# Forgetting attention and a gated feed-forward network: the causal mask made on VectorE, constant products on TensorE up to the first gates, and a new order

## The chip, the cores and the metric

The kernel runs on one core of one Trainium2 chip. The metric is the device time in microseconds of one execution of the whole program, inputs and outputs in the chip's main memory. A core has TensorE (matrix products and transposes, into the accumulation memory PSUM), VectorE, ScalarE, GpSimd and SyncE; the last three issue the transfers here, which run on 16 DMA engines beside the compute engines. In the profile's rows PE is TensorE's products, PEld its weight loads, DVE is VectorE, ACT ScalarE, POOL GpSimd and SP SyncE. Each engine takes its instructions strictly in the order in which the program was written for it.

## The reference, cut to what matters

Attention with a forget gate (8 batches, 8 heads, 576 positions, 64 wide), then a root-mean-square norm and a gated feed-forward network on the 4608 x 512 result:

```python
log_f = np.log(np.clip(f, 0.0001, 1.0))
cum = np.cumsum(log_f, axis=-1)
decay = cum[:, :, :, None] - cum[:, :, None, :]
scores = np.where(causal, -1e9, scale * q @ k.T + decay)      # causal: above the diagonal
attn = softmax(scores)
x = (attn @ v).transpose(0, 2, 1, 3).reshape(4608, 512)
xn = x / np.sqrt(np.mean(x * x, -1, keepdims=True) + 1e-6) * rms_g
g = xn @ w_gate                                               # 512 x 1536
return (g * sigmoid(g) * (xn @ w_val)) @ w_out                # w_out 1536 x 512
```

## The kernel before, in words

**Tiles.** The 576 positions of a batch are four tiles of 128 and a last one of 64. For a tile of queries the kernel turns q and k (on TensorE for the first eight tiles, by a transposing transfer for the others), forms the scores of all eight heads against each key tile (L560), takes the exponential on ScalarE (L600), masks the diagonal tile, multiplies by V (L628) and divides by the sum (L644, L646). The decay is put into V: `Vs` is v times exp(-cum), and the same factor stands as a 65th column for the sum (L531, L532). The factors come from f by a chain at the start: clip (L365), logarithm (L367), running sum on VectorE (L372), exponential (L377), transposes into an accumulation bank (L383), copy to `decT` (L387).

**The mask.** For the tiles of the first group (`FAST`) the mask is added in PSUM ahead of the scores: two products of the identity with `keep` (L571), a 128 x 128 tile that holds 0 up to the diagonal and -1e30 beyond it. `keep` is made by GpSimd at the start (`emit_keep`, L351 and L352). For the other diagonal tiles GpSimd zeroes the exponentials (L608).

**The network.** 36 tiles of 128 tokens make nine groups of 512. Per group 12 gates: eight or four products with w_gate and as many with w_val (L773), tanh (L786), two VectorE steps (L788, L780); then the projection with w_out (L807), a copy out of PSUM (L821) and the store (L829, L838). The first two groups' gates go in halves of two query tiles, so that they start when two tiles are normalized (L679, L686, L699, L706). The last of the 36 tiles is projected in two parts, 384 and 128 columns wide: ScalarE copies the first out, VectorE the second; each part is stored by two transfers, one from SyncE's queue and one from ScalarE's.

**The order.** Nothing is ordered by hand. Each step is a `Unit` with an engine, an assumed duration, a key, what it depends on and which buffers it takes and gives. `Plan.run` plays the program with these assumed durations and has each free engine take the ready unit with the lowest key; the sequence so found is the program's order. `SHIFTS` holds one number per unit; a hundredth of it is added to the unit's key. q, k and weights are loaded from GpSimd's queue (L404, L427, L433), the first four v tiles from SyncE's (L454), later ones from both (L417). At most eight transfers are under way per queue.

**The constant products.** After the third tile of the first group the plan adds ten units with the key 50, each one product of the identity with `keep` into an otherwise unused accumulation bank (L591). With this key TensorE takes one only when nothing else is ready, and `spare = 2` leaves two banks free. Nothing reads what they compute.

Of the kernel before, what the change touches and what calls it, by code (L numbers as in the profile page):

```python
# [9 lines left out]
F32 = mybir.dt.float32  # L10
BF16 = mybir.dt.bfloat16
ALU = mybir.AluOpType
ACT = mybir.ActivationFunctionType
# [890 lines left out]
```

## Time and profile before

| | |
|---|---|
| median of three runs | 374.91 us (373.24, 374.91, 374.98) |
| the profiled execution | 372.92 us, span 371.2 us from its first to its last instruction |
| TensorE's granted clock | 1.000 |
| busy: PE, PEld, DVE, ACT, POOL | 96%, 54%, 62%, 56%, 52% |
| read, written in main memory | 38.16 MB, 9.44 MB |
| first gate product (L773) | 22.46 us after the span's start |
| last projection product (L807) | begins its last twelve at 365.87 us |
| chain that ended last, by engine | PE 83%, DMA 8%, POOL 4%, issue 2% |

A row of the timeline gives the start, the busy time, the engine, the line and what is written from what; in brackets stands how long the engine stood idle before, and what ended that. A row of the waits gives who waited for what: the total in us, how many times, the longest. In the chain of waits each row is a start, a length and the work that the next step waited for. Busy time of TensorE contains the drain of its pipeline, so the sum of its rows is a little more than the time that it stood in anyone's way.

### The profile page before, as it was taken

How to read it: one execution, taken by the hardware profiler on the slowest of the kernel's cores; microseconds unless marked ns; L12 is line 12 of the kernel's file. 1: busy time of each engine (PE TensorE's matmuls, PEld its weight loads, DVE VectorE, ACT ScalarE, POOL GpSimd, SP SyncE). 2: the span in 40 equal slices, each digit the busy share in tenths (PEclk: the TensorE clock that was granted, in tenths of full speed). 3: DMA queues.
4: the chain of work that ended last, by engine and by line, in shares of the span. 5: the costliest groups of instructions: out<-in, count | busy, mean ns of one | idle time of the engine just before them, and what ended most of it. 6: DMA issues, size and time to landing. Idle time of an engine off the chain costs nothing.

```text
span 371.2 us, 8881 instructions
## 1 busy us (share of the span) xinstructions
PE 355.6 (96%) x3539; PEld 201.4 (54%) x3539; DVE 229.4 (62%) x456; ACT 207.8 (56%) x313; POOL 191.2 (52%) x255
## 2 busy tenths in 40 slices
PE   2789999999999989999999999999999999999996
PEld 1567866878554555545554555455444554444443
DVE  5587666787666774775735978646664536777200
ACT  4683666777556857775666658467426633332221
POOL 8885999959988725964743478573000210000000
PEclk9999999999999999999999999999999999999999
DMA  9999999999999995999599499993301030000024
GB/s 112 196 204 201 215 211 152 194 140 146 127 165 195 159 125 123 123 175 140 84 166 190 61 132 158 190 143 70 105 2 57 15 116 30 1 1 2 21 98 107
DMA packets 157017, 45.03 MB, mean 121 GB/s; under 512 B 145520, under 2 KB 151408, under 8 KB 156976
## 3 DMA queue, kind: packets, MB, share of 16 engines
q0 software_dynamic: 81952, 17.83, 56.4%
q1 hardware_dynamic: 74864, 26.51, 38.7%
q8 instruction: 27, 0.44, 0.5%
q10 hardware_dynamic: 160, 0.13, 0.2%
q14 instruction: 14, 0.11, 0.1%
HBM read 38.16 MB, written 9.44 MB: 128 GB/s over the span
## 4 chain that ended last, share of the span: by engine, by line
PE 83%; DMA 8%; POOL 4%; issue 2%; DVE 1%; SPq 1%; ACT 0%; POOLq 0%; ACTq 0%
PE ff L773 45%; PE ff L807 26%; PE sc L560 6%; PE ff L628 6%; DMA qk<-in_k_dram 3%; DMA v<-in_v_dram 2%; DMA wv<-in_moe_w_val_dram 2%; POOL qk L404 2%; POOL Vs L531 1%; PE ff L510 1%; DVE xn L690 0%; PE ff L591 0%; POOL keep L352 0%; SPq L496 0%; PE ff L699 0%
## 5 line engine op out<-in xcount | busy, mean ns | idle before, releaser
L600 ACT ACTIVATE PT<-sc 128x1024 bf16<-128x1024 f32 x100 | 98.5, 1021 | 37.9 <-PE sc L560 34.0
L807 PE MATMUL ff<-wo,hT 128*128 128x512 bf16 (+2 forms) x444 | 104.7, 373 | 0.2
L788 DVE SCALAR_TENSOR_TENSOR ga<-th,ff 128x512 f32<-128x512 f32 x108 | 73.6, 685 | 48.7 <-ACT th L786 45.4
L786 ACT ACTIVATE th<-ff 128x512 f32<-128x512 f32 x108 | 64.3, 599 | 60.5 <-PE ff L773 54.6
L773 PE MATMUL ff<-xT,wv 128*128 128x512 bf16 (+1 forms) x480 | 94.5, 337 | 0.3 <-DMA wv<-in_moe_w_val_dram 0.3
L773 PE MATMUL ff<-xT,wg 128*128 128x512 bf16 (+1 forms) x480 | 93.8, 337 | 0.1
L780 DVE SCALAR_TENSOR_TENSOR hT<-ga,ff 128x512 bf16<-128x512 f32 x108 | 72.3, 684 | 18.6 <-PE ff L773 16.0
L773 PEld LDWEIGHTS <-wg 128*128 128x128 bf16 x528 | 50.1, 98 | 41.2 <-issue 0.2
L773 PEld LDWEIGHTS <-wv 128*128 128x128 bf16 x528 | 49.4, 98 | 39.1 <-DMA wv<-in_moe_w_val_dram 0.5
L807 PEld LDWEIGHTS <-hT 128*128 128x128 bf16 x444 | 40.0, 98 | 40.5 <-issue 0.4
L608 POOL TENSOR_SCALAR_AFFINE_SELECT PT<-PT 128x1024 bf16<-128x1024 bf16 x32 | 36.5, 1145 | 49.0 <-ACT PT L600 48.8
L531 POOL TENSOR_TENSOR Vs<-v,decT 128x512 bf16<-128x512 f32 (+1 forms) x37 | 40.2, 1088 | 27.0 <-DMA v<-in_v_dram 26.4
L821 ACT COPY ores<-ff 128x512 f32<-128x512 f32 (+1 forms) x36 | 21.0, 583 | 36.5 <-PE ff L807 36.5
L628 PEld LDWEIGHTS <-PT 128*128 128x128 bf16 (+1 forms) x960 | 32.4, 103 | 15.3 <-ACT PT L600 2.4
L628 PE MATMUL ff<-Vs,PT 128*128 128x65 bf16 (+1 forms) x960 | 36.2, 195 | 3.1 <-ACT PT L600 1.5
L404 POOL DMA_DIRECT2D qk<-in_q_dram x40 | 35.2, 882 | 0.8 <-POOLq L888 0.8
L404 POOL DMA_DIRECT2D qk<-in_k_dram x40 | 34.8, 872 | 0.7 <-PE ff L773 0.4
L679 POOL TENSOR_TENSOR rs<-ms,mhalf 128x1 f32<-128x1 f32 (+1 forms) x28 | 17.2, 614 | 29.4 <-ACT junk L660 24.3
L560 PEld LDWEIGHTS <-KT 64*128 64x128 bf16 x960 | 23.9, 95 | 15.5 <-issue 14.4
L560 PE MATMUL sc<-QT,KT 64*128 64x128 bf16 (+1 forms) x960 | 32.1, 210 | 0.1
L646 DVE TENSOR_TENSOR x<-ff,rden 128x256 f32<-128x256 f32 x72 | 30.6, 424 | 2.5
L690 DVE SCALAR_TENSOR_TENSOR xn<-x,rs,rgB 128x512 bf16<-128x512 f32 x28 | 23.2, 836 | 12.4 <-POOL rs L679 12.2
(58 smaller groups left out, 163.0 us busy)
## 6 DMA issues: line engine op xcount, KB each, us to landing
out_dram<-ores SPq DMA_DIRECT2D x32, 256.0 KB, 2.5
v<-in_v_dram SPq DMA_DIRECT2D x20, 256.0 KB, 5.4
qk<-in_q_dram POOLq DMA_DIRECT2D x32, 128.0 KB, 6.2
qk<-in_k_dram POOLq DMA_DIRECT2D x32, 128.0 KB, 5.9
v<-in_v_dram POOLq DMA_DIRECT2D x12, 256.0 KB, 6.8
wo<-in_moe_w_out_dram POOLq DMA_DIRECT2D x2, 768.0 KB, 12.4
wg<-in_moe_w_gate_dram POOLq DMA_DIRECT2D x2, 512.0 KB, 12.1
wv<-in_moe_w_val_dram POOLq DMA_DIRECT2D x2, 512.0 KB, 13.0
```

Of the source, the lines that this page charges most:

```text
L404: nc.gpsimd.dma_start(out=T_qk[h.slot][0:n, :].rearrange("p (h d) -> p h d", d=D), in_=src[b, :, p0:p0 + n, :].rearrange("h p d -> p h d"))
L531: eng.tensor_tensor(T_Vs[hv.slot][0:n, j, :, 0:D], T_v32[h.slot][0:n, :, :], bcast(dj, D), ALU.mult)
L560: nc.tensor.matmul(t[:, par, c:c + n], lhsT=kt[r, p, kj * 128:(kj + 1) * 128], rhs=qt[r, p, qi * 128:qi * 128 + n], start=(b, qi) not in FAST,
L600: nc.scalar.activation(T_PT[hp.slot].rearrange("p (a c) -> p a c", a=2), T_sc[h.slot], ACT.Exp, scale=scale)
L608: nc.gpsimd.affine_select(out=d, in_=d, pattern=[[0, 1024 // n], [1, n]], compare_op=ALU.is_ge, fill=0.0, base=0, channel_multiplier=-1)
L628: nc.tensor.matmul(po[i * n:(i + 1) * n, p, :], lhsT=T_PT[h.slot][:, c:c + n], rhs=T_Vs[hold_Vs[x].slot][:, kj, 2 * p + par, :], start=(kj ...
L646: nc.vector.tensor_tensor(d, po[:, :, 0:D], bcast(rden[par], D), ALU.mult)
L773: nc.tensor.matmul(T_ff[h.slot][:, c:c + n], lhsT=w[:, dc, fc * 128:(fc + 1) * 128], rhs=xT[:, dc, t0:t0 + n], start=(dc == 0), stop=(dc = ...
L780: nc.vector.scalar_tensor_tensor(hT, in0=three[0], scalar=0.5, in1=three[1], op0=ALU.mult, op1=ALU.mult)
L786: th = act(0.6, key - 0.1, lambda: nc.scalar.activation(T_th[ht.slot], T_ff[hg.slot], ACT.Tanh, scale=0.5), [ug], take=[ht])
L788: a = dve(0.72, key - 0.1, lambda: nc.vector.scalar_tensor_tensor(T_ga[ha.slot], in0=T_th[ht.slot], scalar=1.0, in1=T_ff[hg.slot], op0=ALU ...
L807: nc.tensor.matmul(T_ff[hf.slot][:, 0:wide], lhsT=T_hT[hold_hT[g].slot][:, fc, j * 128:(j + 1) * 128], rhs=wo[:, fc, cols], start=(fc == 0 ...
```

## The change

`keep` is now made on VectorE: a running sum of the identity's rows along the free dimension gives 1 from the diagonal on and 0 before it, and one further pass takes off 1 and multiplies by 1e30. There are 24 constant products instead of 10; the first becomes ready when `keep` is there, and those that the plan would place after the first gate are planned but not written into the program (`gates_on`). The first part of the last tile's result is copied by VectorE, and both of its stores go through ScalarE's queue. Some assumed durations of the planner are other, and all of `SHIFTS` is new, so the order is new in the whole kernel.

```diff
 SHIFTS = (
-    0, 0, 0, 0, 105, 0, 233, 0, -21, 138, -2, -97, -143, 99, -68, -7, -156, -83, 68, 67, 271, 121, 109, -61, -136,
...
+    192, 80, -10, -64, -70, -114, 28, 12, 26, 20, 201, -61, -93, 228, 95, 185, -84, 23, 386, -127, -102, 35, -147,
...
 )
...
+    upto = sb.tile([128, 128], F32, name="upto")
+    one128 = sb.tile([128, 1], F32, name="one128")
...
     def emit_keep():
-        nc.gpsimd.memset(keep, 0.0)
-        nc.gpsimd.affine_select(out=keep, in_=keep, pattern=[[1, 128]], compare_op=ALU.is_ge, fill=-1.0e30, base=0,
-                                channel_multiplier=-1)
+        ones = bass.AP(tensor=one128.tensor, offset=one128.offset, ap=[one128.ap[0], [0, 128]])
+        nc.vector.tensor_tensor_scan(upto, ones, ident_f, 0.0, ALU.mult, ALU.add)
+        nc.vector.tensor_scalar(keep, in0=upto, scalar1=-1.0, op0=ALU.add, scalar2=1.0e30, op1=ALU.mult)
...
     def emit_ones():
         nc.vector.memset(unit, 1.0)
+        nc.vector.memset(one128, 1.0)
...
-    keeps = pool(0.65, -28.5, emit_keep)
...
+    keeps = dve(0.5, -39.9, emit_keep, [iden_f])
     d3 = dve(1.75, -40, emit_cum, [d2])
...
-            qkload[b, nm, j] = load("POOL", 0.9 * n / 128, (8 * n, 0.0009), key, emit, take=[h])
+            qkload[b, nm, j] = load("POOL", 0.9 * n / 128, (8 * n, 0.00105 if j == 0 and b < WAVE else 0.0009), key, emit, take=[h])
...
-            vload[b, 0] = load("SP", 0.95, (1024, 0.00117), -30 + 0.1 * b, emit, [t])
+            vload[b, 0] = load("SP", 0.95, (1024, 0.00102), -30 + 0.1 * b, emit, [t])
...
-            u = pe(0.42 if b + j * WAVE < 4 else 0.25, key, emit, [iden, qkload[b, nm, j]], take=[h], give=[hq])
+            u = pe(0.42 if b + j * WAVE < 2 else 0.27, key, emit, [iden, qkload[b, nm, j]], take=[h], give=[hq])
...
+    gates_on, go = [], [iden, keeps]
+    for i in range(24):
+        h1 = Hold("ff", 1)
+
+        def fill(h1=h1):
+            if not gates_on:
+                m = bass.AP(tensor=keep.tensor, offset=keep.offset, ap=[keep.ap[0], [0, 4], [1, 128]])
+                nc.tensor.matmul(T_ff[h1.slot], lhsT=ident, rhs=m, start=True, stop=True)
+        go = [pe(0.43 if i < 10 else 0.24, 50, fill, go, take=[h1], give=[h1])]
+        go[0].lat = 0.0
+        go[0].spare = 2
...
-            u = pe(0.86, key - 0.6, bias, [iden, keeps] + ([last_bias[0]] if last_bias[0] else []), take=[h0])
+            u = pe(0.86 if tiles[0][0] < 2 else 0.46, key - 0.6, bias, [iden, keeps] + ([last_bias[0]] if last_bias[0] else []), take=[h0])
...
-        u = pe(0.19 + 0.25 * cols, key, emit, deps, take=holds, give=gives)
+        u = pe(0.19 + 0.25 * cols - (0.1 if tiles[0][:2] in FAST else 0.0), key, emit, deps, take=holds, give=gives)
         last_block[0] = u
-        if len(fast) == 3 and fast[-1] is holds:
-            go = [u]
-            for _ in range(10):
...
-                go = [pe(0.3, 50, fill, go, take=[h1], give=[h1])]
-                go[0].spare = 2
...
-            cost = 1.42 if qi == LAST else 0.03 + (0.12 if qi else 0.22) * (qi + 1)
+            cost = 1.42 if qi == LAST else 0.03 + 0.12 * (qi + 1)
...
-                t = pe(0.25 if g else 0.42, key, tr, [u, iden], take=[hf], give=[hn])
+                t = pe(0.25 if g else 0.27, key, tr, [u, iden], take=[hf], give=[hn])
...
         def mm(w, h):
+            gates_on.append(g)
             xT = T_of[g][hx.slot]
...
-            add, copy = (dve, nc.vector.tensor_copy) if x else (act, nc.scalar.copy)
+            add, copy = (dve, nc.vector.tensor_copy) if halves == 2 else (act, nc.scalar.copy)
...
-                eng, queue = ("ACT", nc.scalar) if j == 3 and i == 1 else ("SP", nc.sync)
+                eng, queue = ("ACT", nc.scalar) if j == 3 and (x == 0 or i == 1) else ("SP", nc.sync)
```

More of the change, by code (lines that the diff above doesn't have):

```diff
@@ L541, in tiles_of @@
         return [(((x, 2 * i), (x, 2 * i + 1)), 64) for x in (b, b + 1) for i in range(2)] + [(((b, LAST), (b + 1, LAST)), 64)]
-    hold_PT, masked, last_block, last_bias, fast = {}, {}, [None], [None], []
+    hold_PT, masked, last_block, last_bias = {}, {}, [None], [None]
     FAST = {(b, qi) for b in range(B) for qi in range(LAST) if home(b, qi)[0] == 0}
@@ L571, in bias @@
                     nc.tensor.matmul(T_sc[h0.slot][:, par, :], lhsT=ident, rhs=m, start=True, stop=False)
-            u = pe(0.86, key - 0.6, bias, [iden, keeps] + ([last_bias[0]] if last_bias[0] else []), take=[h0])
+            u = pe(0.86 if tiles[0][0] < 2 else 0.46, key - 0.6, bias, [iden, keeps] + ([last_bias[0]] if last_bias[0] else []), take=[h0])
             last_bias[0] = u
             deps.append(u)
-            fast.append(holds)
         for b, qi, items, n in tiles:
@@ L581, in score_block @@
         cols = sum(len(items) * n / 128 for b, qi, items, n in tiles)
-        u = pe(0.19 + 0.25 * cols, key, emit, deps, take=holds, give=gives)
+        u = pe(0.19 + 0.25 * cols - (0.1 if tiles[0][:2] in FAST else 0.0), key, emit, deps, take=holds, give=gives)
         last_block[0] = u
-        if len(fast) == 3 and fast[-1] is holds:
-            go = [u]
-            for _ in range(10):
-                h1 = Hold("ff", 1)
-                def fill(h1=h1):
-                    m = bass.AP(tensor=keep.tensor, offset=keep.offset, ap=[keep.ap[0], [0, 4], [1, 128]])
-                    nc.tensor.matmul(T_ff[h1.slot], lhsT=ident, rhs=m, start=True, stop=True)
-                go = [pe(0.3, 50, fill, go, take=[h1], give=[h1])]
-                go[0].spare = 2
         for (b, qi, items, n), h in zip(tiles, holds):
```

152 rows, old and new, of the table SHIFTS are left out of this document.

## The prediction

> **What bounds the kernel now.** I read the page's span, engine rows and slices first, then the chain of work that ended last, the waits of TensorE, TensorE's busy time in stretches, and the timeline of the first 28 us and the last 7.
>
> ```profile
> span 371.2 us, 8881 instructions
> PE 355.6 (96%) x3539; PEld 201.4 (54%) x3539; DVE 229.4 (62%) x456; ACT 207.8 (56%) x313; POOL 191.2 (52%) x255
> PE   2789999999999989999999999999999999999996
> DMA  9999999999999995999599499993301030000024
> ```
>
> TensorE is busy 96% of the span; its thin slices are the first two or three, one near 135 us and the last. The stretches say how much is idle (first number: length; then PE busy; the last three are TensorE's granted clock, the packets in flight on each DMA engine and GB/s):
>
> ```profile
> 22.00:34.00 12.00, 11.06 (x109) 9.55 (x110) 9.40 (x17) 6.80 (x13) 6.86 (x9) 1.00 1.46 205
> 34.00:46.00 12.00, 11.64 (x153) 9.74 (x151) 7.90 (x16) 6.60 (x9) 10.94 (x14) 1.00 1.56 209
> 46.00:130.00 84.00, 84.00 (x1050) 55.47 (x1049) 59.89 (x123) 56.11 (x76) 74.90 (x98) 1.00 1.58 166
> 130.00:140.00 10.00, 8.57 (x156) 5.09 (x155) 7.30 (x17) 5.29 (x7) 2.74 (x4) 1.00 0.85 118
> 140.00:366.00 226.00, 226.00 (x1969) 112.73 (x1962) 131.30 (x242) 119.49 (x190) 76.50 (x95) 1.00 0.64 92
> ```
>
> From 46 to 366 us TensorE has 1.43 us of idle time in all (10.00 - 8.57, around 135 us); from 22 to 46 it has 0.94 + 0.36 = 1.30. So an order can win at most 2.7 us behind 22 us, and the rest must come from the first 22 us or the tail. It can lose without such a limit.
>
> What holds the start is the chain up to 34 us:
>
> ```profile
> 3.91 1.73 POOL qk L404 x2
> 5.64 0.23 POOL keep L351
> 5.93 1.34 POOL keep L352
> 7.52 2.61 POOL qk L404 x3
> 12.47 8.30 DMA wv<-in_moe_w_val_dram
> 20.77 12.93 DMA qk<-in_k_dram
> ```
>
> GpSimd issues the q and k loads, stops to build the mask (0.23 + 1.34), goes on issuing, and from 12.47 the chain is transfers. TensorE's waits name the same things, and the one of 1.4 us near 135:
>
> ```profile
> PE sc L571 <- POOL keep L352: 1.6, 1, 1.6
> PE ff L628 <- POOL PT L608: 1.4, 1, 1.4
> PE ff L510 <- DMA qk<-in_k_dram: 1.2, 2, 0.7
> ```
>
> **Part 1, the mask goes from GpSimd to VectorE.** GpSimd loses 0.23 + 1.34 = 1.57 us ahead of the third pair's loads. Does the DMA stream move by as much?
>
> ```profile
> 4.00:6.00 2.00, 0.61 (x4) 0.45 (x5) 1.21 (x9) 0.86 (x2) 1.93 (x4) 1.00 1.70 108
> 8.00:10.00 2.00, 2.00 (x11) 1.08 (x9) 0.00 (x0) 1.20 (x2) 2.00 (x3) 1.00 1.62 214
> 10.00:12.00 2.00, 1.28 (x15) 1.04 (x15) 0.42 (x1) 0.64 (x2) 2.00 (x4) 1.00 1.94 203
> 20.00:22.00 2.00, 1.29 (x21) 0.81 (x21) 1.49 (x6) 1.89 (x4) 2.00 (x3) 1.00 1.34 206
> ```
>
> ```profile
> 5.13 5.23 SPq L454 DMA_DIRECT2D v<-in_v_dram  x4
> ```
>
> In the hole that the mask leaves (8 to 10 us) the engines still move 214 GB/s: SyncE's four v loads, issued from 5.13 to 10.36, fill it. From 20 to 22 us the rate stands at 206 GB/s, and from 22 to 34 it is 205. So loads issued 1.57 us sooner mostly change places with v loads. Bounds: 0 (fully swapped) and -1.57 us (the whole delay); I take -0.3, nearest to the row of 8 to 10 us, where 1.62 packets are in flight against 1.94 in the next stretch: a sixth of 2 us is spare.
>
> VectorE gains a scan over 128 elements and a pass of 128x128 from f32 to bf16, and one memset:
>
> ```profile
> 4.45 0.34 DVE L363 CAST ident<-ident_f 128x128 bf16<-128x128 f32 x1
> 5.83 1.35 DVE L372 TENSOR_TENSOR_SCAN hT<-unit,hT 64x576 f32<-64x576 f32 x1 [0.72 <-ACT hT L367]
> 12.14 0.49 DVE L387 COPY decT<-ff 128x320 f32<-128x320 f32 x1 [1.63 <-PE ff L383]
> ```
>
> The scan is 1.35 x 128/576 = 0.30, the cast 0.34, the memset of one column little: about 0.7 us, 0.6 to 1.0. VectorE pauses 0.72 us before the long scan, where most of it fits. If it lies ahead of that scan, the decay chain (scan, exp, transposes, decT) is late by up to 0.7; decT waited 1.63 us for TensorE, so that cover holds: 0. Without it the first scaled V would be 0.7 later, and the first tile's values with it. The mask is there at about 6 instead of 7.27, and TensorE's wait of 1.6 us ends about 1.2 sooner. What is late next is the second k tile:
>
> ```profile
> 10.77 0.61 PE L510 MATMUL ff<-ident,qk 128*128 128x128 bf16 x4 [0.72 <-DMA qk<-in_k_dram]
> ```
>
> It was issued ahead of the mask, so it does not come sooner. The 1.2 us are therefore worth 0 by themselves.
>
> The row of the mask shows something else: on GpSimd the 128x128 select of the identity took 0.29 us, and that of the mask 1.34, under VectorE's scan (5.83 to 7.18).
>
> ```profile
> 3.62 0.29 POOL masks.py:199 TENSOR_SCALAR_AFFINE_SELECT ident_f<-ident_f 128x128 f32<-128x128 f32 x1
> ```
>
> The Trainium skill, "SBUF — State Buffer", section "Who interferes with whom", says that a VectorE instruction with two SBUF inputs excludes a GpSimd one that reads SBUF, and that a VectorE cast can hold off the writing of descriptors for GpSimd's own DMAs. The trace agrees with the first (1.34 against 0.29). By the second, the new cast could hold up a q or k issue by its 0.34 us; that speaks against this part, and would turn its -0.3 into 0.
>
> **Part 2, 24 constant products instead of 10, from the mask on, none after the first gate.** Before, three of the ten lay ahead of the gates (19.1 to 21.2) and seven in the last microseconds. TensorE's rate changes once, about 18 us:
>
> ```profile
> 14.51 1.90 PE L571 MATMUL sc<-keep,ident 128*128 128x512 bf16 x4
> 17.18 0.62 PE L510 MATMUL ff<-ident,qk 128*128 128x128 bf16 x4
> 18.31 0.40 PE L699 MATMUL ff<-ident,xn 128*128 128x128 bf16 x4 [0.52 <-ACT xn L686]
> 21.73 0.68 DVE L706 TENSOR_TENSOR xT<-ff,rgT 128x512 bf16<-128x512 bf16 x1
> 22.46 1.03 PE L773 MATMUL ff<-xT,wg 128*128 128x256 bf16 x8
> 27.86 0.39 PE L773 MATMUL ff<-xT,wv 128*128 128x256 bf16 x2 [0.30 <-DMA wv<-in_moe_w_val_dram]
> ```
>
> Four transposes take 0.62 before and 0.40 after, though the granted clock reads 1.00 throughout. The change came after 14.51 to 18 us, some 3.6 us with hardly a pause (an estimate). With fills from 6 us I expect it at 10 to 13 us. Then the four bias products at 14.51 and the two transposes up to 17.80 halve: about 0.85 + 0.4 = 1.25 us of TensorE's queue that the second tile's values wait behind. Against it: a fill that started just before real work delays it by up to one product's step, 1.90 / 4 = 0.47, in perhaps three pauses that matter, on average half of it: +0.7. So I expect the first gate 0.55 sooner than 22.46, between +0.7 (fills only delay) and -1.25. But the product at 27.86 waits for wv, so a gate that starts sooner is caught there. To the end I carry -0.5 (0 to -1.25), part 1's 0.3 being what makes the weights sooner.
>
> The Trainium skill, "TensorE: Matmul & The Clock Gate", section "What's actually happening", says that the array runs at half rate until a window of about 3.4 us has been busy, that the window runs freely, and that where it begins differs from run to run. The rows agree (0.62 against 0.40 after some 3.6 us).
>
> **Part 3, the tail.**
>
> ```profile
> 365.65 0.21 PE ff L591
> 365.87 0.67 PE ff L807 x12
> 366.24 1.30 ACTq L838 DMA_DIRECT2D out_dram<-ores  x2
> 366.63 0.29 DVE L821 COPY ores<-ff 128x128 f32<-128x128 f32 x1 [20.24 <-PE ff L807]
> 365.69 2.40 SPq L838 DMA_DIRECT2D out_dram<-ores  x4
> ```
>
> ```profile
> L821 ACT COPY ores<-ff 128x384 f32<-128x384 f32 x1 | 0.5, 480 | 0.1
> ```
>
> One fill (0.21) goes from before the last products; the six behind them delayed nothing. The 384-wide copy moves to VectorE: 0.29 + 256 x 1.04 ns (the slope of 0.68 us for 512) = 0.56 against 0.48 on ScalarE. SyncE's last issue ended at 368.09; now ScalarE's queue has three of 0.65, from about 366.3 to 368.2. Sum 0, between -0.4 (SyncE's spare issue) and +0.3.
>
> **Part 4, the new order and the planner's new costs.** They change no instruction's work. They can win at most the 2.7 us above, and lose as much per new wait as the 1.4 at 135 us. I take 0, -2.0 to +3.0.
>
> **Sum.** The profiled execution took 372.92 (span 371.2): -0.3 - 0.5 + 0 + 0 = 372.1. The median shown, 374.91, is 2.0 above it; the three runs are 373.24, 374.91 and 374.98, two groups 1.7 apart. One mechanism fits that distance: if the rate rises some 3.6 us later than here, the first gates (1.03 for eight products with the last one's drain) run at half rate from 22.46 to about 26 and half of 3.6, 1.8 us, are lost. Fills up to the first gates take that away. No row shows a late run, so this is an estimate; it makes the median 372.1 plus the 0.3 by which the fastest of the three lies above the profiled execution: 372.4.
>
> **The rivals.**
> *R1: the start is hidden behind the transfers, and the spread stays.* For it: 206 GB/s from 20 to 22, 205 after, and the wait at 27.86. Then -0.7 remains of the median, 374.2: no change that can be told. "The fills don't do what they say" ends here too: transposes still at 0.62 up to 18 us.
> *R2: the order also clears the wait at 135 us and part of 22 to 46.* Worth another 1.4 to 2.7: 370.5. Against it: nothing in the change gives GpSimd less to do there, where it is busy 74.90 of 84 us.
> *R3, the other side: a new wait for GpSimd behind 46 us.* Place: the values products (L628) behind the mask of PT or the scaling of V, when the order puts a load's issue ahead of either. Price 1.4 each, by the row. With the start as in R1 it decides from 2.6 us, that is two such waits: 374.2 + 2.8 = 377.0. For it: GpSimd's 74.90 of 84 leave little room; against it: before had one such wait in 320 us.
> *R4: 24 fills run out ahead of the gates, and the rate falls again in a pause.* Then the first gates run at half rate as in the estimate above, 1.8 on 372.1: 373.9, with R1's result. For it: 24 fills last 24 x 0.47 = 11 us at the slow step and 5 to 6 at the fast one (0.21), and from 6 to 22 are 16 us; against it: the rate held before through the pauses from 18.31 to 22.46 with three fills. That an idle window closes the array's clock is what the Trainium skill, "TensorE: Matmul & The Clock Gate", states in the same section; no row here shows a fall.
>
> **How the numbers follow.** 0.5% is 1.87 us, about what a measurement of this kernel can tell. Forecast 372.4: 0.42. R1 with R4: 0.33. R2: 0.08. R3: 0.17. Faster: 0.08 and nearly all of the forecast's, 0.48; same: 0.35; slower: 0.17. Range: down to 370.4 (R2, the order's -2.0 on the forecast) and up to 376.0, which leaves most of R3 out. The forecast's own range is 371.3 to 373.5.
>
> **What would show it.** Part 1: no GpSimd mask, TensorE's wait for keep gone, VectorE's scan and cast near 0.30 and 0.34, the wv wait near 27.9 earlier by about 0.3. Part 2: four transposes at 0.40 by 13 us, the first gate near 21.9. Part 3: no L591 at the end, ScalarE's queue last. Part 4: TensorE 84.00 of 84 busy again from 46 to 130. Wrong, if the runs keep their two groups, or if a wait over 1 us stands behind 46 us.

## The result, and the profile after

The changed kernel took 376.21 us (median of 11 runs, 373.6 to 377.9) beside 373.55 for the kernel before (11 runs): a ratio of 1.0064, 95% interval [1.0041, 1.0088]. It is slower by 2.4 us (1.5 to 3.3 by the interval), where 372.4 and "faster" were forecast. Ratios here are taken round by round without disturbed runs, so they aren't always the quotient of the medians. The profiled execution took 375.92 us, 3.0 above the one shown of before; its span is 2.2 longer.

The page of the changed kernel, the lines that answer to those shown of before:

```profile
span 373.4 us, 8833 instructions
PE 353.3 (95%) x3495; PEld 201.8 (54%) x3542; DVE 236.7 (63%) x460; ACT 206.9 (55%) x312; POOL 189.5 (51%) x253
PE   3779999999999999999999899999999999999995
PEclk9699999999999999999999999999999999999999
DMA  9999999999899994999999939991421001100304
```

The thin slice of TensorE near 135 us is gone and one near 210 has come. The second slice of the granted clock reads 6. Its waits:

```profile
PE sc L586 <- DVE keep L355: 5.2, 1, 5.2
PE ff L513 <- DMA qk<-in_q_dram: 1.9, 1, 1.9
PE ff L632 <- POOL PT L612: 1.6, 1, 1.6
PE ff L632 <- DVE Vs L535: 0.6, 1, 0.6
```

The lateness begins at the first gates. From the timeline of the changed kernel, VectorE and then TensorE:

```profile
4.45 0.42 DVE L354 TENSOR_TENSOR_SCAN upto<-one,ident_f 128x128 f32<-128x128 f32 x1
4.90 0.23 DVE L355 TENSOR_SCALAR keep<-upto 128x128 bf16<-128x128 f32 x1
5.04 0.88 DVE L367 TENSOR_SCALAR hT<-hT 64x576 f32<-64x576 f32 x1
5.88 0.08 DVE L454 MEMSET v<- 128x1 f32 x4
21.02 0.69 DVE L534 TENSOR_TENSOR Vs<-v,decT 128x512 bf16<-128x512 f32 x1 [1.32 <-DMA v<-in_v_dram]
25.24 0.68 DVE L710 TENSOR_TENSOR xT<-ff,rgT 128x512 bf16<-128x512 bf16 x1
```

```profile
21.86 0.28 PE L632 MATMUL ff<-Vs,PT 128*128 128x65 bf16 x4 [0.56 <-DVE Vs L535]
25.98 1.03 PE L778 MATMUL ff<-xT,wg 128*128 128x256 bf16 x8 [0.22 <-DVE xT L710]
```

The first gate starts at 25.98 instead of 22.46. Behind it stands the last v tile: VectorE idles 1.32 us for it until 21.02, and the second tile's transposed input (L710) comes behind that on the same queue. That v landed at 21.0, in before at 17.94; the last weight landed at 34.77 instead of 32.84, although GpSimd issued the first at 9.34 instead of 10.11. Counting TensorE's weight loads, each with the columns of its product and without the constant products, the changed kernel reaches the same amount of work about 3.4 us later than before behind the first gates (25 us), 2.3 to 3.2 later from 40 to 130 us, 1.3 to 1.6 later from 138 to 207 (before has its own wait of 1.35 for the mask of PT at 136), 2.4 to 2.9 behind its own wait of 1.65 at 210, and 2.2 at the last product. So the lateness of the start, 2.5 us at 40, is about the whole difference of these two profiled executions, and the two waits for a mask of PT nearly cancel. Nothing is lost in the tail:

```profile
368.31 0.98 DVE L826 COPY ores<-ff 128x384 f32<-128x384 f32 x2 [8.22 <-PE ff L812]
368.90 1.85 ACTq L843 DMA_DIRECT2D out_dram<-ores  x3
```

What the transfers did shows in stretches of the start, before and then after (the last three numbers are the granted clock, the packets in flight per DMA engine and GB/s):

```profile
4.00:8.00 4.00, 1.28 (x6) 0.70 (x7) 3.02 (x12) 2.17 (x3) 3.93 (x12) 1.00 1.66 146
8.00:12.00 4.00, 3.28 (x25) 2.12 (x24) 0.42 (x1) 1.84 (x3) 4.00 (x6) 1.00 1.78 208
12.00:16.00 4.00, 3.30 (x31) 2.13 (x28) 2.96 (x10) 2.52 (x3) 3.49 (x5) 1.00 1.80 188
16.00:20.00 4.00, 3.36 (x35) 2.15 (x33) 3.12 (x10) 3.56 (x7) 3.06 (x6) 1.00 1.60 190
```

```profile
4.00:8.00 4.00, 2.82 (x12) 1.53 (x13) 3.21 (x10) 2.01 (x3) 4.00 (x12) 1.00 1.75 116
8.00:12.00 4.00, 2.51 (x27) 1.44 (x24) 1.94 (x7) 3.37 (x6) 4.00 (x6) 1.00 1.54 179
12.00:16.00 4.00, 2.76 (x23) 1.67 (x24) 1.73 (x6) 0.31 (x2) 1.85 (x3) 0.55 1.83 166
16.00:20.00 4.00, 4.00 (x35) 2.52 (x33) 2.16 (x7) 2.63 (x5) 2.50 (x4) 0.60 1.36 183
```

The rate is lower in each: 30 + 29 + 22 + 7 = 88 GB/s for 4 us is 0.35 MB, which at 205 GB/s is 1.7 us, near the 1.93 by which the weights are late. From 16 to 20 us the two queues carry this (GpSimd's q0, mostly weights; q1, mostly SyncE's v), again before, then after:

```profile
q0 software_dynamic: 2062, 0.75, 158.2%
q1 hardware_dynamic: 31, 0.01, 1.5%
```

```profile
q0 software_dynamic: 1043, 0.48, 89.4%
q1 hardware_dynamic: 985, 0.25, 47.0%
```

Before, v was nearly over by then: its last tile landed at 17.94. In the changed kernel v's packets of some 256 bytes go one for one with those of the other queue (985 and 1043).

### The profile page after: what moved, and what is told of

The parts are those of the page before. It is cut to its first block, busy times and chain, and to the rows that moved or that the text cites. A ratio compares the mean times of both kernels' runs of the same rounds, so it can differ in the third digit from the quotient of the medians.

```text
span 373.4 us, 8833 instructions
## 1 busy us (share of the span) xinstructions
PE 353.3 (95%) x3495; PEld 201.8 (54%) x3542; DVE 236.7 (63%) x460; ACT 206.9 (55%) x312; POOL 189.5 (51%) x253
## 4 chain that ended last, share of the span: by engine, by line
PE 71%; POOL 10%; DMA 10%; issue 4%; SPq 3%; DVE 1%; ACT 0%; POOLq 0%; DVEq 0%
PE ff L778 39%; PE ff L812 21%; PE ff L632 5%; PE sc L575 5%; POOL qk L407 5%; DMA qk<-in_q_dram 4%; DMA wv<-in_moe_w_val_dram 3%; DMA v<-in_v_dram 3%; POOL Vs L534 2%; SPq L499 2%; SPq L714 1%; POOL PT L612 1%; POOL v L420 1%; POOL Vs L535 1%; POOL rs L683 1%
## 5 line engine op out<-in xcount | busy, mean ns | idle before, releaser
L812 PE MATMUL ff<-wo,hT 128*128 128x512 bf16 (+2 forms) x425 | 100.1, 373 | 1.4 <-issue 0.5
L778 PE MATMUL ff<-xT,wv 128*128 128x512 bf16 (+1 forms) x465 | 93.5, 335 | 0.8 <-issue 0.2
L778 PE MATMUL ff<-xT,wg 128*128 128x512 bf16 (+1 forms) x469 | 92.6, 336 | 0.9 <-DVE xT L710 0.2
L812 PEld LDWEIGHTS <-hT 128*128 128x128 bf16 x444 | 40.8, 98 | 42.9
L826 ACT COPY ores<-ff 128x512 f32<-128x512 f32 x35 | 20.4, 589 | 32.3 <-PE ff L812 30.3
L694 DVE SCALAR_TENSOR_TENSOR xn<-x,rs,rgB 128x512 bf16<-128x512 f32 x28 | 27.4, 993 | 13.8 <-POOL rs L683 13.7
## 6 DMA issues: line engine op xcount, KB each, us to landing
wo<-in_moe_w_out_dram POOLq DMA_DIRECT2D x2, 768.0 KB, 12.4
```

Source lines behind the costliest of these rows:

```text
L778: nc.tensor.matmul(T_ff[h.slot][:, c:c + n], lhsT=w[:, dc, fc * 128:(fc + 1) * 128], rhs=xT[:, dc, t0:t0 + n], start=(dc == 0), stop=(dc = ...
L812: nc.tensor.matmul(T_ff[hf.slot][:, 0:wide], lhsT=T_hT[hold_hT[g].slot][:, fc, j * 128:(j + 1) * 128], rhs=wo[:, fc, cols], start=(fc == 0 ...
```

## The experiments

Three theories are told apart. M, mixing: GpSimd's old mask was the gap in which SyncE's v loads went through; without it, and with v issued later, v rides beside q, k and the weights. Q: the new order loads the second tile's q fifth instead of third. O: the new order as a whole. Some expectations name more: V, VectorE's scan and cast themselves cost the time; C, the clock; S, a wait near 208 us; N, a cost of the new order in the middle. The code is shortened: `place` and `swap` stand for lines that move steps in the finished order, `...` for lines left out, and the comments are added. The numbers of all kernels, from their traces and runs ("GpSimd pauses" is whether it does other work of about 1.6 us ahead of its later loads; times of landing and of the gate are of one profiled execution each; a_no_fill has six runs, the others 11 or 12):

| kernel | GpSimd pauses | q1 packets, 16-20 us | last v, last weight land | first gate | ratio to before [95%] |
|---|---|---|---|---|---|
| before | yes | 31 | 17.94, 32.84 | 22.46 | 1 |
| after | no | 985 | 21.0, 34.77 | 25.98 | 1.0064 [1.0041, 1.0088] |
| a_v_first | no | 333 | 18.68, 33.78 | 23.88 | 1.0069 [1.0044, 1.0094] |
| a_q1_first | no | 987 | 20.83, 35.15 | 25.86 | 1.0050 [1.0023, 1.0076] |
| a_pool_held | yes | 365 | 18.53, 32.93 | 23.57 | 1.0042 [1.0018, 1.0067] |
| a_start3 | yes | 31 | 17.25, 33.14 | 23.80 | 1.0043 [1.0005, 1.0081] |
| a_no_fill | no | 873 | 20.35, 34.45 | 25.64 | 1.0118 [1.0075, 1.0162] |
| a_gps_mask | yes | 40 | 17.25, 33.09 | 24.41 | 1.0020 [0.9990, 1.0049] |
| b_mask_dve | no | 833 | 19.27, 33.99 | 23.50 | 1.0018 [1.0000, 1.0036] |
| b_mask_dve_held | yes | 91 | 18.33, 33.24 | 22.71 | 1.0008 [0.9978, 1.0038] |
| b_all | no | 854 | 20.00, 33.97 | 24.35 | 1.0061 [1.0032, 1.0090] |
| b_tail | yes | 57 | 17.87, 32.79 | 22.57 | 0.9987 [0.9962, 1.0011] |
| b_fill | yes | 85 | 17.87, 32.80 | 23.08 | 0.9980 [0.9957, 1.0003] |
| b_best | yes | 3 | 16.41, 33.09 | 22.97 | 1.0011 [0.9986, 1.0037] |

**a_v_first**: the changed kernel, with the clip and the four one-column memsets that release v's loads ahead of the mask's scan on VectorE.

```diff
-        for u in P.run():
+        order = P.run()
...
+        place([d1] + early_v, keeps)      # before the mask
+        for u in order:
```

> The changed kernel with VectorE's clip of f and the four one-column memsets that release SyncE's v loads put back ahead of the mask's scan; all else in its order. Theory M (mixing): the v loads, issued 0.85 us later than before and now beside q and k loads, reach into the weights' transfer and slow it; with the v loads back at about 5.1 us the last v tile should land near 20 instead of 21.0, the last w_val near 34.2 instead of 34.8, the end 0.5 us sooner. Theory Q (load order): the second tile's q, loaded fifth and landing at 13.2, sets the first gate at 26.0; it stays fifth here, so the first gate stays within 0.4 us of 26.0 and the time within 0.3 us of the changed kernel.

The start was repaired by 2.1 us at the first gate, and the time not at all: 376.38. The work was 1.4 us late at 40 us, then more was lost near 208. GpSimd's and TensorE's timeline and the stretches there:

```profile
208.22 1.04 POOL L542 TENSOR_TENSOR Vs<-v,decT 128x512 bf16<-128x512 f32 x1 [7.41 <-DMA v<-in_v_dram]
209.35 1.09 POOL L620 TENSOR_SCALAR_AFFINE_SELECT PT<-PT 128x1024 bf16<-128x1024 bf16 x1
210.50 0.57 PE L640 MATMUL ff<-Vs,PT 128*128 128x65 bf16 x13 [2.62 <-POOL PT L620]
```

```profile
208.00:212.00 4.00, 1.50 (x16) 0.81 (x17) 1.11 (x4) 1.43 (x2) 3.40 (x5) 0.89 1.39 167
212.00:216.00 4.00, 4.00 (x49) 2.25 (x48) 2.45 (x6) 1.19 (x3) 0.71 (x1) 0.69 0.17 33
```

A late v holds GpSimd, its next mask comes late, TensorE stands 2.62 us; then the granted clock falls to half for 3.4 us (211.1 to 214.5 in the trace): four 512-wide products take 1.73 us at 210.90, and 1.03 at 206.09.

**a_q1_first**: the second tile's q is loaded third, the third tile's k fifth; their transposes and copies change places too.

```diff
-        for u in P.run():
+        order = P.run()
...
+        swap(order, issues[2, "k", 0], issues[1, "q", 0])     # and turns, copies
+        for u in order:
```

> The changed kernel with the second tile's q loaded third, as before, and the third tile's k fifth, and the two turns on TensorE and their copies moved likewise (the third tile's k is turned just ahead of its q). Theory Q: q lands near 8 instead of 13.2, TensorE's wait of 1.9 us for it goes, the second tile's scores come near 11.5 instead of 15.1, the first gate near 23 to 24 instead of 26.0 (w_gate lands at 22.0), and the end 1.5 to 2.5 us sooner, that is level with before. Theory M: the weights still land as late (last w_val near 34.8), the gates that start sooner wait for them, and the end is at most 0.5 us sooner.

The wait of 1.89 for q went, the first gate did not move; v was as late as ever, and the wait turned up there:

```profile
21.69 0.28 PE L640 MATMUL ff<-Vs,PT 128*128 128x65 bf16 x4 [1.81 <-DVE Vs L543]
25.86 1.70 PE L786 MATMUL ff<-xT,wg 128*128 128x256 bf16 x8
```

Theory Q falls as the cause by itself. The first eight gate products took 1.70 instead of 1.03: the clock had closed at 23.8.

**a_pool_held**: GpSimd is kept busy as before by a memset and a select on a tile that nobody reads.

```diff
+        nc.gpsimd.memset(spare, 0.0)
+        nc.gpsimd.affine_select(out=spare, in_=spare, ...)
         nc.gpsimd.memset(mhalf, -0.5)
...
```

> The changed kernel with GpSimd held for as long as the mask held it before (a memset and a select into a spare tile nobody reads, ahead of its other constants). Theory M: q and k from the fifth load on are issued 1.6 us later, the v loads pass in the gap, the last v lands near 18 to 19 instead of 21.0 and the last w_val near 33 to 33.5 instead of 34.8; the end 1 us sooner although the engine does more. Theory Q: the second tile's q is issued later and lands no sooner than 13.2, first gate 26 or later, end 0 to 1 us later.

To issue the weights later by 0.8 us made them land 1.84 us sooner (32.93 against 34.77), v 2.5 sooner, the gate 2.4 sooner, though again at half rate. That is theory M's sign. The time did not follow: the ratio, 1.0042, is lower than the change's, but the intervals overlap.

**b_mask_dve** and **b_mask_dve_held**: the kernel before with part 1 alone, the mask behind the memsets that release v, so that v is issued on time; and the same with GpSimd held.

```diff
-        nc.gpsimd.memset(keep, 0.0)
-        nc.gpsimd.affine_select(out=keep, in_=keep, ...)
+        nc.vector.tensor_tensor_scan(upto, ones, ident_f, 0.0, ALU.mult, ALU.add)
+        nc.vector.tensor_scalar(keep, in0=upto, scalar1=-1.0, op0=ALU.add, scalar2=1.0e30, op1=ALU.mult)
```

> The kernel before with the mask alone moved to VectorE, behind the memsets that release the v loads; the rest in the order of before (ten constant products, tail as before). The prediction's part 1: -0.3 us (0 to -1.57). Theory M: the gap in GpSimd's issues is gone, v tiles land 1 us or more later than in before (17.9 for the last), the last weight later than 32.8, the end 0.5 to 1.5 us later than before. Theory Q: the load order is that of before, so the first gate is at 22.5 or a little sooner and the end level or up to 0.5 us sooner.

> The kernel before with the mask on VectorE and GpSimd held as long as its mask held it (memset and select into a spare tile). Theory M: the gap in GpSimd's issues is back, v tiles pass in it: last v near 18, last weight near 32.9, time level with before within 0.3 us although VectorE does more. Theory V: VectorE's scan and cast are what costs; then it stays 0.5 to 1 us above before like the kernel with the mask alone moved (1.0018).

This pair is one edit apart, with before's order. The queues from 16 to 20 us, first not held, then held:

```profile
q0 software_dynamic: 1602, 0.50, 112.3%
q1 hardware_dynamic: 833, 0.21, 39.8%
```

```profile
q0 software_dynamic: 2179, 0.73, 159.6%
q1 hardware_dynamic: 91, 0.02, 4.2%
```

A pause of 1.57 us on GpSimd takes v out of the weights' way, and the weights land 0.75 us sooner. Over the table the split has no exception: with a pause the last weight is there by 33.24, without one never before 33.78. So theory M stands for the transfers. It does not follow for the first gate of this pair, which starts 0.8 us sooner when held. The two run level up to 18.5 us, and VectorE waits for no v in either; then one has a closed clock until 22.88 and the other an open one from 18.05, here by the same four transposes, not held and then held:

```profile
18.53 0.61 PE L702 MATMUL ff<-ident,xn 128*128 128x128 bf16 x4 [0.52 <-ACT xn L689]
18.56 0.40 PE L706 MATMUL ff<-ident,xn 128*128 128x128 bf16 x4 [0.51 <-ACT xn L693]
```

That is the clock's part. In time the pair is 1.0018 and 1.0008, which doesn't tell them apart; v issued on time, part 1 costs at most 0.36%. Theory V isn't excluded, but held, with scan and cast on VectorE, it can cost at most 0.38%.

**a_start3**: all three edits of the start in the changed kernel.

```diff
+        place([d1] + early_v, keeps)
...
+        swap(order, issues[2, "k", 0], issues[1, "q", 0])     # and turns, copies
...
+        nc.gpsimd.affine_select(out=spare, in_=spare, ...)    # behind its memset
```

> The changed kernel with all three edits of its start together: v loads released ahead of the mask's scan, the second tile's q loaded third, GpSimd held for 1.57 us by a select into a spare tile. If the start is what costs (theories M and Q), the last v lands near 18, the last w_val near 32.9, the first gate is at 22 to 23 and TensorE's work up to 60 us is level with before within 0.5 us. Theory S: a second cost lies in the new order near 208 us, where values wait for GpSimd's mask behind a late v; by S this wait grows as TensorE comes there sooner (it was 1.8 us in the changed kernel and 4.7 with its clock closing in the kernel with early v loads), so that the time stays 1 to 2 us above before although the start is level. Without S: 374 or less, level with before.

The start is repaired to 0.75 us of work at 40 us, though the first gate, at 23.80, misses the 22 to 23 expected. The time isn't repaired: two waits stand in the middle that the changed kernel's profile does not have. Theory S named another place, near 208 us, and there nothing is lost.

```profile
85.69 1.91 PE L790 MATMUL ff<-xT,wg 128*128 128x256 bf16 x16 [1.81 <-DVE ga L805]
108.35 1.02 PE L790 MATMUL ff<-xT,wg 128*128 128x512 bf16 x4 [2.02 <-DMA xT<-xn]
```

**a_no_fill**: the 13 constant products are left out.

```diff
-    gates_on, go = [], [iden, keeps]
+    gates_on, go = [0], [iden, keeps]
```

> The changed kernel with none of the 13 constant products that it writes into the program; every other instruction in its place. Prediction's part 2: the clock opens later, the first gate comes up to 0.55 us later than with them, time +0 to +0.5. Theory C (clock): the fills opened it at 9.0 in the changed kernel but left a pause in which it closed at 12.4 and opened again at 19.2; without them it opens once, between 17 and 23, and the time is within 0.5 us of the changed kernel. If fills only delay real work: 0.5 us sooner.

```profile
25.64 1.86 PE L778 MATMUL ff<-xT,wg 128*128 128x256 bf16 x8 [1.17 <-DVE xT L710]
```

The clock opened at 30.05 and the gates began at half rate; the work was 4.3 us late at 40 us instead of 2.5. These 1.8 us are the price that the prediction estimated for a late clock, and the times agree (1.0118 against 1.0064, 2.0 us, from six runs; the intervals overlap a little).

**b_tail**: the kernel before with the new tail and without the seven late fills.

```diff
...                                           # no constant products behind the first gate
-            add, copy = (dve, nc.vector.tensor_copy) if x else (act, nc.scalar.copy)
+            add, copy = (dve, nc.vector.tensor_copy) if halves == 2 else (act, nc.scalar.copy)
...
-                eng, queue = ("ACT", nc.scalar) if j == 3 and i == 1 else ("SP", nc.sync)
+                eng, queue = ("ACT", nc.scalar) if j == 3 and (x == 0 or i == 1) else ("SP", nc.sync)
```

> The kernel before with two things alone: the seven constant products behind the first gate are left out, and the last tile's first part is copied by VectorE and stored from ScalarE's queue alone. The prediction said 0 (-0.4 to +0.3). From the two traces the time from the last projection product on is 0.2 shorter and 0.2 of fill goes: -0.4 us, a ratio of 0.999.

0.9987 [0.9962, 1.0011]: no difference. Its profiled execution shows something else. Up to the last microseconds it is the program of before, and yet it lost 3.8 us near 109, where before's profile lost none, and its clock opened at 10.62 instead of 17.87 (and was closed again from 17.45 to 20.86):

```profile
10.96 0.40 PE L510 MATMUL ff<-ident,qk 128*128 128x128 bf16 x4 [0.94 <-DMA qk<-in_k_dram]
22.57 1.03 PE L776 MATMUL ff<-xT,wg 128*128 128x256 bf16 x8
```

So one program can differ by that much from execution to execution, and a wait in the middle of a single profile can't be charged to an edit. The open clock did not make the first gate sooner: 22.57 against 22.46.

**b_all** and **b_fill**: before's order of everything. b_fill has GpSimd's mask, eight more fills set ahead of the early transposes and values, no late ones, and the new tail. b_all has the mask on VectorE ahead of the clip as well, as the change has it, and two fills more.

```diff
...
+        order.remove(keeps)                       # b_all alone
+        order.insert(order.index(d1), keeps)      # b_all alone
+        for ref, n_ in ((turns[1, "q", 0], 2),    # b_all alone
+                        (turns[1, "k", 0], 2), (vals[0, 0][0], 3), (trs[0, 0], 2), (vals[1, 0][0], 1)):
+            # n_ constant products ahead of ref
```

> Everything of the change but its new order: the kernel before, in its own order and load order, with the mask on VectorE ahead of the clip of f (as in the changed kernel), 13 constant products (ten of them put by hand ahead of the turns and values that pause, three as before) and none after the first gate, and the new tail. If the new order costs nothing, this is as slow as the changed kernel, ratio 1.006. Theory O (the order, with its loads, is the larger part): 1.000 to 1.002, that is the mask's +0.9 us of the kernel with the mask alone, less the tail's 0.4.

> The kernel before with its mask on GpSimd, eight more constant products put ahead of the second tile's k turn, the first values and the first transposed tiles, none after the first gate, and the new tail. Theory C: the clock opens by 15 us and is open when the gates start; the start is then set by the weights' transfer as before, so the time is that of the kernel with the tail alone, ratio 0.998 to 0.999, with fewer high runs. If fills delay real work: 1.000 to 1.002.

Run side by side they differ clearly: 1.0061 [1.0032, 1.0090] and 0.9980 [0.9957, 1.0003]. They differ in part 1 and in two fills; b_best, below, has these two fills as well and is level with before. Part 1 as it was made is therefore enough for a loss as large as the change's, without the new order, and the fills and the tail without it lose nothing. VectorE and the first gate of b_all, then the first gate of b_fill:

```profile
17.36 0.70 DVE L542 TENSOR_TENSOR Vs<-v,decT 128x512 bf16<-128x512 f32 x1 [2.38 <-DMA v<-in_v_dram]
24.35 1.03 PE L791 MATMUL ff<-xT,wg 128*128 128x256 bf16 x8
```

```profile
23.08 1.03 PE L788 MATMUL ff<-xT,wg 128*128 128x256 bf16 x8 [0.25 <-DVE xT L720]
```

Theory O, that it takes the new order to lose, falls. The third v tile landed at 17.34 here, at 15.63 in b_mask_dve, where v was issued 0.9 us sooner and VectorE waited for none, and at 12.52 in before: the lost pause and the late issue add up. One thing stays open: the profiled execution of b_all was its fastest, 374.15, and 1.2 us longer in span than before's; where its other runs (median 375.50) lose the rest no trace shows.

**b_best**: b_fill's edits and two fills more, with the mask on VectorE behind the memsets and GpSimd held.

```diff
+        nc.vector.tensor_tensor_scan(upto, ones, ident_f, 0.0, ALU.mult, ALU.add)     # and the pass to keep
...
+        nc.gpsimd.affine_select(out=spare, in_=spare, ...)                            # behind its memset
...
+        for ref, n_ in ((turns[1, "q", 0], 2), ...):                                  # as in b_all
```

> The same with the mask on VectorE behind the memsets that release the v loads and GpSimd held as long as before, with two products more ahead of the second tile's q turn. The mask is there at about 5.7 us, so the clock opens by 11 to 13; v and weights land as in before (theory M). Expected 0.997 to 0.999; the loads still set the first gate at 22 to 22.7.

1.0011 [0.9986, 1.0037]. With the same fills as b_all, it has v on time and the pause, and b_all's loss is gone (the intervals overlap between 1.0032 and 1.0037). No kernel here is clearly faster than the one before; b_fill comes nearest.

**a_gps_mask**: the changed kernel with part 1 alone undone.

```diff
-        nc.vector.tensor_tensor_scan(upto, ones, ident_f, 0.0, ALU.mult, ALU.add)
-        nc.vector.tensor_scalar(keep, in0=upto, scalar1=-1.0, op0=ALU.add, scalar2=1.0e30, op1=ALU.mult)
+        nc.gpsimd.memset(keep, 0.0)               # between its fourth and fifth load
+        nc.gpsimd.affine_select(out=keep, in_=keep, ...)
```

> The changed kernel with its first part alone undone: the mask is made by GpSimd again, between the fourth and the fifth of its loads, and VectorE has neither scan nor cast. The new order of every other step, the 13 fills and the new tail stay. If part 1 is the whole loss (theory M: without GpSimd's gap the v loads ride beside the weights), the last v lands by 18.5 us, the last weights by 33.3, the first gate starts at 22.5 to 23.6 (the second tile's q is still the fifth load, 1.6 us later than in the changed kernel) and the time is 0.998 to 1.001 of before. If the new order costs something of its own in the middle (theory N), the start is repaired in the same way and the time still is 1.003 to 1.005. If neither (the order of the loads alone holds the start), the first gate stands at 25 us or later and the time is 1.006.

```profile
q0 software_dynamic: 1676, 0.77, 146.5%
q1 hardware_dynamic: 40, 0.01, 1.9%
```

v and weights came back as theory M says (17.25 and 33.09). The first gate, at 24.41, is later than expected: the second tile's q still held TensorE 0.95 us at 13.43, so the order of loads has its share once v is out of the way. The work is 0.9 late at 40 us instead of 2.5. The ratio, 1.0020 [0.9990, 1.0049], lies between theory M's and theory N's and decides neither; its interval overlaps the change's.

## Why the prediction was wrong, point by point

**Part 1 is the step that failed.** It was given -0.3, between 0 and -1.57, from the row of 8 to 10 us at 214 GB/s: "loads issued 1.57 us sooner mostly change places with v loads". The swap was seen, the sign of its price not. An exchange was taken to cost nothing at worst ("0 (fully swapped)"). But the bytes went through more slowly (166 GB/s against 188 from 12 to 16 us), and the exchange put the small, soon-needed v behind or beside weights that nobody needed before the first gates. The bounds left no room for a loss, and no reason was given that excluded one. Measured, part 1 as it was made costs 1.4 us by the medians and 3.0 by the ratios between b_all and b_fill, and 1.3 and 1.9 between b_all and b_best, which differ only in the place of the mask and in the pause. Between the change and a_gps_mask it is 1.6 by the ratios, and where v was issued on time (b_mask_dve) 0.7, neither clear of noise; that 0.7 holds the clock's part too.

The way from the start to the whole time is shown only in part. Three kernels with v back early (a_v_first, a_pool_held, a_start3) have their first gate at 23.6 to 23.9 and still 1.0042 to 1.0069. So something besides the late v costs time in these three, and what it is stays open.

The second half of the miss is the wait that the new work adds, which the prediction put at 0. It asked whether 0.7 us on VectorE would delay the decay chain, and found cover in TensorE's wait. It did not ask what else was queued behind it: the four memsets that release v's loads stand behind the scan, the cast and the clip, which took 0.88 us. SyncE issued the first v at 5.98 instead of 5.13. Scan and cast themselves took 0.42 and 0.23, as expected in sum (0.65 against "about 0.7").

The Trainium skill, "DMA: Bandwidth & Descriptors", section "Queues, rings and completion order", says that a DMA engine takes turns between the queues with work, packet by packet. By that rule late v packets take turns with the weights' instead of waiting behind them; the trace agrees, with 985 packets against 1043 in 4 us. The other rule weighed in the prediction, that VectorE's cast could hold up GpSimd's issues, did not show: they took 0.89 each beside the scan (3.86, two in 1.78), as before.

**Part 2.** Half right. The fills opened the clock early, four transposes take 0.40 at 10.08; but it closed again (12.4 to 19.2, the 0.55 and 0.60 of the stretches), in the pause of 1.89 for q. That is R4's mechanism, ahead of the gates in the changed kernel and at them in a_q1_first and a_pool_held. The step from an early clock to an early gate fails in before's order: b_tail's clock was open from 10.62 to 17.45 and again from 20.86, and its first gate came at 22.57, not 0.55 sooner. When the clock opens isn't fixed either, as b_tail and before differ by 7 us with one and the same start. Thirteen of the 24 were written. In the new order they earn some 2 us (a_no_fill); in before's order they earn nothing that can be told (b_fill 0.9980, b_tail 0.9987). The reading of the three times as two groups 1.7 apart, which made the forecast 372.4, was not borne out: seventeen later times of before, taken beside a_gps_mask, have no gap over 0.6 us between 372.8 and 375.0. It carried most of the forecast: of the 2.5 us from 374.91 to 372.4 the parts give 0.8 and the two groups 1.7. With 11 runs the median of before is 373.55, so 1.4 of the 2.5 was never there to be won. Between b_tail and before the distance of two executions lay near 109 us and not at the first gates.

**Part 3.** Right: 0 forecast, 0.9987 [0.9962, 1.0011] measured in b_tail, late fills included. From the start of the last copy to the end of the span are 4.38 us, in before 4.57.

**Part 4.** 0 forecast, -2.0 to +3.0; open within that. a_gps_mask has the order, 13 fills and the tail, b_fill 11 fills and the tail: 1.0020 and 0.9980, some 1.5 us for the order, with overlapping intervals. 0.9 us of it can be seen at 40 us in a_gps_mask. What it costs in the middle isn't settled: the waits at 85, 109 and 208 us come and go from profile to profile, and one at 109 comes in before's order too (b_tail).

**The rivals.** R1 had the right place, transfers hold the start, but not that they could get later. R3 named the other side at the wrong place: the changed kernel has one such wait behind 46 us, of 1.65 at 210 us, in the place of the one of 1.35 at 136. A wait over 1 us there was one of the prediction's signs of being wrong, though before had one too. R2's clearing of the wait at 135 was seen and paid back at 210. A slip in the sums decides nothing: R1's 0.7 is 0.8 by the terms (0.3 and 0.5).

## What to carry to other kernels

When two queues share the DMA engines, a pause in one of them may be what lets the other's urgent loads through: before filling such a gap, write down for each load when it is needed, and price the swap on both sides of zero. When work is put on an in-order engine, list everything queued behind it, one-column memsets that release a transfer included. A gain at the start is kept only if the waits further on stay as they were; measure parts in pairs one edit apart, side by side, and look at more than one profiled execution before charging a wait to an edit.

## What the runs showed of the hardware

A pause of TensorE of about 2 us in the middle of the kernel can be followed by a closed clock for 3.4 us, and need not be. Here are two kernels, first b_tail (timeline and stretch), then b_best:

```profile
108.93 2.94 PE L776 MATMUL ff<-xT,wg 128*128 128x512 bf16 x8 [1.98 <-DVE x L648]
108.00:112.00 4.00, 3.07 (x9) 1.16 (x10) 2.08 (x5) 0.63 (x2) 2.61 (x4) 0.70 1.59 193
```

```profile
110.10 1.89 PE L795 MATMUL ff<-xT,wg 128*128 128x512 bf16 x7 [2.12 <-DVE rden L664]
108.00:112.00 4.00, 1.85 (x8) 0.91 (x10) 2.95 (x6) 0.60 (x1) 2.70 (x5) 1.00 2.26 177
```

After 1.98 us it closed (0.70), after 2.12 it did not (1.00). Once it has opened, every closed stretch in these traces that ends before the program does lasts 3.4 us or twice that. The Trainium skill, "TensorE: Matmul & The Clock Gate", section "What's actually happening", gives a window of about 3.4 us that runs freely and an idle window that closes the clock; the lengths agree, and a free-running window would explain why pauses of one size differ and why one program's clock opened at 10.62 (b_tail) and at 17.87 (before); no run here tests it by itself. So a wait of this size costs its length, or up to 1.7 us more, half of 3.4.

The granted clock reads 1.00 in the records until its first change, though products ran at half rate: in before's profile 1.00 from the start, with four transposes still at 0.62 at 17.18; the first change is recorded at 17.87.
